# A long convolution's transform as 64 by 32 points in place of 128 by 16, with both parts of a split in one contraction

## The chip, the core and the metric

The kernel runs on one core of a Trainium2 chip. The core has engines with a queue of instructions each: TensorE (PE, matrix products; its weight loads are listed as PEld), VectorE (DVE), ScalarE (ACT), GpSimd (POOL) and SyncE (SP, which here only issues transfers). Each works through its queue in order and waits for the others by semaphores. The metric is the device time of one execution in microseconds; lower is better.

## What is computed

Four sublayers on x with S = 2048 rows and D = 576 columns, in fp32. Twice: a Fourier mixing, then a gated convolution.

```python
def _A_ref(x, dft_seq_re, dft_seq_im, dft_hid_re, dft_hid_im):
    a = einsum("bsd,ed->bse", x, dft_hid_re)
    b = einsum("bsd,ed->bse", x, dft_hid_im)
    return einsum("ts,bse->bte", dft_seq_re, a) - einsum("ts,bse->bte", dft_seq_im, b)

def _B_ref(q, k, v, shift_k, ssm_k, ssm_D):
    k_shift = ...          # short causal convolution of k, 4 taps per channel
    kv = k_shift * v
    y = irfft(rfft(pad(kv)) * rfft(pad(ssm_k)))[:, :S]   # causal, length 2S, per channel
    return q * (y + kv * ssm_D)

x = x + _A_ref(layernorm(x), ...)
x = x + _B_ref(layernorm(x), k, v, shift_k, ssm_k, ssm_D)
x = x + _A_ref(layernorm(x), ...)
x = x + _B_ref(layernorm(x), k, v, shift_k, ssm_k, ssm_D)
```

The filtered signal y depends on k, v, shift_k, ssm_k and ssm_D alone, not on x. It is computed once and used in both gated sublayers. In the text, this part is "the branch".

## The kernel before

**Precision.** A product of fp32 values is made of values rounded to a shorter form (`float32r`). An operand is split into a high part, rounded by ScalarE, and a low part, the rest, by VectorE (`split`, lines 93 to 95): one ScalarE copy and one VectorE subtraction. A product is then three matmuls: high by high, high by low and low by high.

**The main loop.** `layer` (lines 308 to 346) makes the first mixing as 128 steps: four blocks of 512 output columns (tb), real and imaginary part (g), 16 slices of rows (k). A step takes one 128x512 tile of the DFT matrix, the "c tile". `load_c` loads and splits it two steps ahead, into a ring of three tiles (`ring["cs"]`). The step then issues 12 matmuls of 512 columns into four accumulators (`s`) and two into a fifth (`rm`). For the first 16 steps, rows of x are normalised on the way (`get_x0`). At the end of a block's half, `evac_u` and `evac_r` take the accumulators to tiles u. Once both halves of a block are there, `hidden` (lines 274 to 297) makes the products with the matrices w, which `load_w` loads and splits from step 41 (`W_FROM`) on.

**The branch** runs in between, as a generator that the main loop advances (lines 798 to 823). It has three stages.

- *The first stage*, up to `f1_products`, transforms the zero-padded signals over 128 points spaced 16 rows apart, for each of the 16 phases j: once for the filter ssm_k (src 1), once for the product kv (src 0). That makes 32 row tiles of 128 partitions x 576 columns. `convolve` (lines 389 to 404) makes the shifted k for two phases at a time, seven VectorE operations on tiles of 1152 columns. `f1_split` (lines 433 to 443) multiplies by v for src 0 and splits the row tile into the ring xf of three tiles, that lie in the region `f1r` with the constants fc. `f1_products` (lines 445 to 456) makes, for each half of the columns (288) and for real and imaginary part, three matmuls into one of three PSUM banks `bk` and a ScalarE copy out, and then stores the two parts to t_d in memory. The products follow the splits by one or two row tiles (`F1_LAG`). From step 16 to step 42 (`F1_END`) about one row tile is taken per main step, and the convolution is issued at the pace at which its results fall due (lines 472 to 484).
- *The middle stage* reads t_d in 37 pieces, 128 rows by 504 columns for both signals (or the columns left over), transforms over the 16 phases with one 128x128 matrix, multiplies the two spectra, transforms back and stores to v_d. Its loads begin at step 45 (`MID_LOAD`), its products at step 47.
- *The second inverse stage* loads v_d by phase (`load_row`), splits it, and makes for each phase and each half of the columns six matmuls (`i2_products`), which go to the tensors yb_d.

After this, `make_x1` and `gated` use yb_d for both gated sublayers, and a second mixing follows with fewer block products.

**What sets the order.** Nothing is written out by hand: the tile framework puts the instructions of each engine in an order before the run, by readiness in a model of its own and by the place in the program. `behind` and `issue_after` only add "not ahead of that instruction on this engine". On the chip, every engine keeps that order. So a c tile's low half on VectorE can stand behind convolution work and splits of the branch, and a main step on TensorE cannot begin before its c tile's two halves are there.

Of the kernel before, what the change touches and what calls it, by code (L numbers as in the profile page):

```python
# [10 lines left out]
F32 = mybir.dt.float32  # L11
FR = mybir.dt.float32r
AF = mybir.ActivationFunctionType
OP = mybir.AluOpType

P = 128
S = 2048
D = 576
J = S // P
TB = 4  # L20
NT = 512
HD = D // 2
NC = 4
REM = D - NC * P
EPS = 1e-5
# [16 lines left out]
MW = 504  # L42
# [8 lines left out]
KP = 4  # L51
H = 2 * P
WIDE = 2 * NT
# [14 lines left out]
def fnet_h3_kernel(ctx: ExitStack, tc: tile.TileContext, x, c_mat, w_re, w_im, k_pad, v, shift_k,  # L68
                   ssm_k, ssm_d, f1c, i2c, midc, out):
    nc = tc.nc  # L70
# [3 lines left out]
    dr = ctx.enter_context(tc.tile_pool(name="dr", bufs=1, space=bass.MemoryType.DRAM))  # L74

    def mm(ps, lhsT, rhs, first, last, more=False):
        nc.tensor.matmul(ps, lhsT, rhs, start=first, stop=last, skip_group_check=more)  # L77
# [15 lines left out]
    def split(h, l, src):  # L93
        a = nc.scalar.activation(h, src, AF.Copy).ins  # L94
        return a, nc.vector.tensor_tensor(l, src, h.bitcast(F32), OP.subtract).ins  # L95
# [68 lines left out]
    anchor, made, rounded, pows, biased, halved, added, evac, parted, stored = [], [], [], [], [], [], [], [], [], []  # L164

    def load_after(dst, src):
        with tc.issue_after(anchor[-1]):
            return nc.sync.dma_start(dst, src).ins
# [31 lines left out]
        made.append(nc.vector.tensor_tensor(t[:, D + REM:], y[:, :NC * P], h[:, :NC * P], OP.subtract).ins)  # L200
        return t

    t_d = dr.tile([P, J, 2, 2, D], F32, name="t")
    v_d = dr.tile([P, J, 2, D], F32, name="vd")
    yb_d = [dr.tile([P, D], F32, name=f"yb{j}") for j in range(J)]
    xa_d = [dr.tile([P, D], F32, name=f"xa{j}") for j in range(J)]
    xb_d = [dr.tile([P, D], F32, name=f"xb{j}") for j in range(J)]
# [147 lines left out]
    def branch():  # L355
        f1r = region_b(FR, "f1r")
        lay(f1r, 0, ("xf", 2 * D, 3), ("fc", 4 * P, 5))
        at = lay(flts, SC_AT + CRAW * NT, ("so", D, 4), ("land", D, 3))
        lay(flts, at, ("craw", NT, 1))
        f1f = region_a(F32, "f1f")  # L360
        ks = f1f[:, :KR * 2 * D]
        lay(f1f, KR * 2 * D, ("wt", 2 * D, 2), ("rp", 2 * D, 2))
        tmp = f1f[:, 8 * 2 * D:]
        wt, rows, landed, fcs = [], {}, {}, {}
# [68 lines left out]
        def f1_split(j, src):  # L433
            r = landed.pop((j, src))
            if not src:
                row = rows[j // 2][:, j % 2, :]
                nc.vector.tensor_tensor(row, row, r, OP.mult)
                r = row
            elif j == 0:
                nc.vector.tensor_tensor(r[:1], r[:1], tmp[:1, D:], OP.add)  # L440
            xf = parts("xf")
            parted[:] = split(xf[0], xf[1], r)
            return xf

        def f1_products(j, src, xf, fc):
            for hf in range(2):
                so = two(ring["so"]())
                cs = slice(hf * HD, (hf + 1) * HD)
                for c in range(2):
# [4 lines left out]
                    stored[:] = [nc.scalar.activation(so[:, c, :], ps[:, :HD], AF.Copy).ins]  # L454
                nc.scalar.dma_start(t_d[:, j, :, src, cs], so)
                yield

        conv, made_ops, split_up, share = convolve(), 0, [], 0.0
        for n, (j, src) in enumerate(todo):
# [3 lines left out]
            xf = f1_split(j, src)  # L463
# [48 lines left out]

        RW = D - MW
        per = MW // RW
        groups = P // 4
# [6 lines left out]
        def load_mid(n):  # L522
            if n < len(mids):
                first, count = mids[n]
                w = width(n)
                landed[n] = [r[:, :w] for r in apart] if n % 2 else [ring["land"]()[:, :2 * w]]
                ends = landed[n] if n % 2 else [two(landed[n][0])[:, i] for i in range(2)]
                src = t_d[4 * first:4 * (first + count)]
                if n < groups:
                    src = src.rearrange("q j c s d -> (q j c) s d")[:, :, :MW]  # L530
                    if n % 2:
                        for i in range(2):
                            load_after(ends[i], src[:, i])
                    else:
                        load_after(two(landed[n][0]), src)
                else:
                    src = src.rearrange("(g q) j c s d -> (q j c) s g d", q=4)
# [41 lines left out]
        def mid_inverse(n, yf):  # L579
            w = width(n)  # L580
            pv = bank()
            mm(pv[:, :w], mc[:, 2, :], yf[0], True, False)
            mm(pv[:, :w], mc[:, 2, :], yf[1], False, False)
            mm(pv[:, :w], mc[:, 3, :], yf[0], False, True)
            vo = ring["vo"]()[:, :w]
            act(vo, pv[:, :w], AF.Copy)
            first, count = mids[n]
            dst = v_d[4 * first:4 * (first + count)]
            if n < groups:
                nc.scalar.dma_start(dst.rearrange("q j c d -> (q j c) d")[:, :MW], vo)  # L590
            else:
                nc.scalar.dma_start(dst.rearrange("(g q) j c d -> (q j c) g d", q=4)[:, :, MW:],
                                    vo.rearrange("p (g d) -> p g d", g=count))

        landed, halves, fcs = {}, {}, {}
# [48 lines left out]
        def i2_products(hf, j, fc, vf):  # L644
            yo = ring["vo"]()
            ps = bank()
            for c in range(2):
                cs = slice(c * D + hf * HD, c * D + (hf + 1) * HD)
                mm(ps[:, :HD], fc[:, c, :], vf[0][:, cs], c == 0, False)
                mm(ps[:, :HD], fc[:, c, :], vf[1][:, cs], False, False)  # L650
                mm(ps[:, :HD], fc[:, 2 + c, :], vf[0][:, cs], False, c == 1)
# [12 lines left out]
        for j in range(J):  # L664
            vf, fc = halves.pop(j), fcs.pop(j)
# [132 lines left out]
    for n, whole in layer(get_x0, lambda j: x[:, j, :], done0, pending):  # L798
        if (whole or whole is not None and n % J < J - 1) and n <= F1_END:
            at = n if whole else n - 0.5  # L800
# [27 lines left out]
        m = n - PREP  # L828
# [132 lines left out]
    cs, done = {}, []  # L961
# [68 lines left out]
    for n, whole in layer(get_x1, lambda j: xb_d[j], done1, pending, 1):  # L1030
# [42 lines left out]
    for ch in range(9):  # L1073
        first, then = (ch + 4, ch + 6) if ch < 4 else (12, ch + 15) if ch < 8 else (22, 24)
# [27 lines left out]
def _parts(a):  # L1102
    h = _r11(a)
    return h, _r11(a - h.astype(np.float64))


def _constants():
    p, q, j, r = np.arange(P), np.arange(P), np.arange(J), np.arange(J)
    n = (16 * p[None, :, None] + j[:, None, None]) * (4 * q[None, None, :] + 1) % 8192
    ang = 2 * np.pi * n / 8192  # L1110
    f1 = [_parts(np.cos(ang)), _parts(-np.sin(ang))]
    f1c = np.stack([f1[0][0], f1[1][0], f1[0][1], f1[1][1]], axis=2)
    at = ang.transpose(0, 2, 1)
    i2 = [_parts(np.cos(at) / S), _parts(-np.sin(at) / S)]
    i2c = np.stack([i2[0][0], i2[1][0], i2[0][1], i2[1][1]], axis=2)
    th = 2 * np.pi * (j[:, None] * r[None, :] % J) / J
    f2 = np.zeros((4, J, 2, 2, 4, J))
    i1 = np.zeros((2, 4, J, 4, J, 2))
    c, s = np.cos(th), np.sin(th)
    for a in range(4):  # L1120
        f2[a, :, 0, 0, a, :] = c
        f2[a, :, 1, 0, a, :] = s
        f2[a, :, 0, 1, a, :] = -s
        f2[a, :, 1, 1, a, :] = c
        i1[0, a, :, a, :, 0] = c.T
        i1[1, a, :, a, :, 0] = -s.T
        i1[0, a, :, a, :, 1] = s.T
        i1[1, a, :, a, :, 1] = c.T
    m = [*_parts(f2.reshape(P, P)), *_parts(i1.reshape(P, P))]
    return f1c, i2c, np.stack(m, axis=1)  # L1130


# [34 lines left out]
```

## Time and profile before

| | |
|---|---|
| median of 3 runs | 1190.47 us (1190.42 to 1191.18) |
| profiled execution | 1190.62 us, span of its instructions 1188.8 us |
| TensorE busy | 1172.7 us, 99% |
| VectorE busy | 814.3 us, 68% |
| ScalarE busy | 614.6 us, 52% |
| first and last product of the first stage | 6.8 and 199.4 us |
| granted TensorE clock | 0.999 |

In the rows of groups and of the timeline, a line stands for the source line of the kernel, then the engine, the operation and the tiles as output<-inputs. A tile of a region carries the region's name: the split rows and the constants of the first stage are `f1r`, c tiles are `mats`, their raw form `flts`, the convolution's tiles `f1f`. In a group, `xcount | busy, mean` is followed by the idle time of the engine just before these instructions and what ended it. In a timeline, the first number is the start and the second the duration, both in microseconds, and x6 means six instructions in a row. In a window, each engine has its busy microseconds and, in brackets, its instructions; then come the granted clock, the share of the DMA engines and GB/s.

### The profile page before, as it was taken

To read this page: it belongs to the slowest core of one execution; us is meant where nothing else is said; L and a number is where in the kernel's file an instruction comes from. 1 tells how busy PE (TensorE), PEld (TensorE's weight loads), DVE (VectorE), ACT (ScalarE), POOL (GpSimd) and SP (SyncE) were. 2 spreads that over 40 slices of the span, in tenths; PEclk is the share of its full clock that TensorE was granted. 3 is DMA by queue.
4 is the path that set the end of the run, shared out by engine and by line. 5 is a ranking of instruction groups with operands and counts; after the bars stand their busy time and mean duration, and the time that the engine had idled before them with its cause. 6 is when DMAs were issued, how large, how long until landed. Compare 5 with 4: busy or idle time off the path is not lost.

```text
span 1188.8 us, 17284 instructions
## 1 busy us (share of the span) xinstructions
PE 1172.7 (99%) x6077; PEld 1013.5 (85%) x6077; DVE 814.3 (68%) x1335; ACT 614.6 (52%) x1106; POOL 66.2 (6%) x100
## 2 busy tenths in 40 slices
PE   7999999999999999999999999999999999999997
PEld 6888888887788888889988898888888888889997
DVE  7899794677677677753447765874775776874764
ACT  7965665466656566644535656634434435540200
POOL 2200000000000000001101111000000000001111
PEclk9999999999999999999999999999999999999999
DMA  9889898545576546459957786872582597696621
GB/s 338 295 266 308 262 297 251 187 151 183 176 236 200 176 137 181 116 160 295 294 164 260 241 262 216 263 261 72 179 315 82 159 326 274 199 335 201 217 94 41
DMA packets 153770, 257.71 MB, mean 217 GB/s; under 512 B 27601, under 2 KB 68817, under 8 KB 153682
## 3 DMA queue, kind: packets, MB, share of 16 engines
q1 hardware_dynamic: 113074, 205.58, 53.7%
q10 hardware_dynamic: 36000, 42.63, 10.3%
q0 software_dynamic: 4608, 8.39, 2.6%
q8 instruction: 48, 0.79, 0.3%
q14 instruction: 40, 0.33, 0.1%
HBM read 189.89 MB, written 66.65 MB: 216 GB/s over the span
## 4 chain that ended last, share of the span: by engine, by line
PE 95%; DVE 2%; DMA 1%; ACT 1%; issue 0%; POOL 0%; POOLq 0%; SPq 0%; DVEq 0%; ACTq 0%
PE s L77 54%; PE bk L77 35%; PE rm L77 6%; DMA flts<-in_c_mat 1%; ACT flts L506 0%; DMA flts<-in_ssm_k 0%; DVE flts L183 0%; DVE u L95 0%; ACT mid L506 0%; DVE mats L95 0%; DVE mats L200 0%; ACT mats L197 0%; ACT u L94 0%; DVE mid L511 0%; POOL flts L186 0%
## 5 line engine op out<-in xcount | busy, mean ns | idle before, releaser
L77 PE MATMUL s<-mats 128*128 128x512 f32 x2088 | 524.1, 392 | 0.8 <-ACT mats L94 0.6
L77 PEld LDWEIGHTS s<-mats 128*128 128x128 f32 x2088 | 386.8, 188 | 79.8 <-DVE u L95 1.5
L95 DVE TENSOR_TENSOR mats<-flts,mats 128x512 fp32r<-128x512 f32 x201 | 137.5, 688 | 80.7 <-ACT mats L94 78.1
L94 ACT ACTIVATE mats<-flts 128x512 fp32r<-128x512 f32 x201 | 125.7, 627 | 102.5 <-PE bk L77 31.3
L506 ACT ACTIVATE flts<-bk 64x504 f32<-64x504 f32 (+3 forms) x180 | 99.0, 550 | 82.9 <-PE bk L77 76.4
L77 PEld LDWEIGHTS bk<-w,u 128*128 128x128 f32 x864 | 117.8, 188 | 4.7 <-ACT flts L506 1.3
L77 PE MATMUL bk<-w,u 128*128 128x288 f32 x864 | 120.5, 295 | 0.5 <-ACT flts L506 0.5
L77 PE MATMUL bk<-mid 128*128 128x504 f32 (+1 forms) x525 | 120.1, 356 | 0.7 <-ACT flts L506 0.2
L511 DVE TENSOR_TENSOR mid<-flts,mid 128x1008 fp32r<-128x1008 f32 (+3 forms) x90 | 80.3, 902 | 45.6 <-ACT mid L506 45.5
L77 PEld LDWEIGHTS bk<-mid 128*128 128x128 f32 x525 | 88.0, 188 | 16.7 <-ACT flts L506 1.8
L77 PE MATMUL rm<-mats 128*128 128x512 f32 x304 | 94.5, 390 | 0.0
L506 ACT ACTIVATE mid<-flts 128x1008 fp32r<-128x1008 f32 (+3 forms) x90 | 71.9, 799 | 37.2 <-DMA flts<-vd 14.2
L454 ACT ACTIVATE flts<-bk 128x288 f32<-128x288 f32 x128 | 50.7, 410 | 48.8 <-PE bk L77 48.3
L77 PE MATMUL bk<-f1r 128*128 128x288 f32 x384 | 64.7, 301 | 7.4 <-ACT f1r L94 6.8
L77 PEld LDWEIGHTS bk<-f1r 128*128 128x128 f32 x384 | 59.9, 192 | 13.9 <-ACT f1r L94 6.8
L77 PE MATMUL bk<-mats 128*128 128x288 f32 (+1 forms) x376 | 67.8, 317 | 0.0
L77 PEld LDWEIGHTS rm<-mats 128*128 128x128 f32 x304 | 57.0, 188 | 12.3
L77 PE MATMUL s<-t,mats 128*128 128x512 f32 x264 | 64.9, 389 | 0.0
L292 DVE TENSOR_TENSOR flts<-flts,bk 128x288 f32<-128x288 f32 x48 | 21.8, 453 | 61.5 <-PE bk L77 61.3
L77 PE MATMUL bk<-mats,t 128*128 128x288 f32 (+1 forms) x368 | 59.3, 303 | 0.0
L186 POOL TENSOR_TENSOR flts<-flts 128x1 f32<-128x1 f32 x35 | 30.1, 860 | 522.1 <-DVE flts L185 518.8
L77 PEld LDWEIGHTS bk<-mats 128*128 128x128 f32 x376 | 55.5, 188 | 3.4
(149 smaller groups left out, 1432.1 us busy)
## 6 DMA issues: line engine op xcount, KB each, us to landing
flts<-in_c_mat SPq DMA_DIRECT2D x148, 256.0 KB, 3.9
ph<-in_c_mat SPq DMA_DIRECT2D x54, 512.0 KB, 4.0
t<-flts ACTq DMA_DIRECT2D x64, 288.0 KB, 4.7
flts<-in_c_mat SPq DMA_DIRECT2D x30, 512.0 KB, 5.1
flts<-vd SPq DMA_DIRECT2D x16, 576.0 KB, 5.1
vd<-flts ACTq DMA_DIRECT2D x36, 252.0 KB, 2.9
flts<-t SPq DMA_DIRECT2D x16, 504.0 KB, 4.0
ud<-ph ACTq DMA_DIRECT2D x12, 512.0 KB, 5.3
```

Source lines behind the costliest of these rows:

```text
L77: nc.tensor.matmul(ps, lhsT, rhs, start=first, stop=last, skip_group_check=more)
L94: a = nc.scalar.activation(h, src, AF.Copy).ins
L95: return a, nc.vector.tensor_tensor(l, src, h.bitcast(F32), OP.subtract).ins
L186: pows.append(nc.gpsimd.tensor_tensor(rs, ve, mhalf, OP.pow).ins)
L292: added[:] = [nc.vector.tensor_tensor(rows[hf], rows[hf], ps[:, :HD], OP.add).ins]
L454: stored[:] = [nc.scalar.activation(so[:, c, :], ps[:, :HD], AF.Copy).ins]
L506: last_act.append(nc.scalar.activation(*args, **kw).ins)
L511: nc.vector.tensor_tensor(l, src, h.bitcast(F32), OP.subtract)
```

## The change

The transform of 2048 points is cut in 64 by 32 in place of 128 by 16. A row tile of 128 partitions now holds two phases, j and 16 + j, of 64 points each: the host lays out k, v and ssm_k so that the even groups of 16 rows lie in partitions 0 to 63 and the odd ones in 64 to 127 (`halves`). The contraction has 64 points, and the 128 rows of the matmul are filled with the high part of a phase and its low part. For each of the two phases b, a tile xf[b] holds the high part in the phase's own half of the partitions and the low part in the other half, and the constant's high part stands in both halves. One matmul so makes high by high and high by low. The second takes the constant's low part, and makes low by high and low by low. So `f1_products` has two matmuls per group, not three, and `f1_split` splits each half of the partitions by itself. Real and imaginary part come out in one product, as 64 frequencies x 2.

The middle stage transforms over 32 phases, on pieces of two frequencies in place of four, with the same tile sizes. In the second inverse stage the six matmuls stay; their constants are now half zeros, as each of the two phases fills 64 of the 128 output rows, and both are summed into one bank. The rows of v_d come in two runs per partition in place of one.

```diff
+Q = P // 2
...
-    t_d = dr.tile([P, J, 2, 2, D], F32, name="t")
-    v_d = dr.tile([P, J, 2, D], F32, name="vd")
+    t_d = dr.tile([Q, 2, 2 * J, 2, D], F32, name="t")
+    v_d = dr.tile([Q, 2, 2 * J, D], F32, name="vd")
...
-                nc.sync.dma_start(ks[:, at:at + 2 * D],
-                                  bass.AP(tensor=k_pad.tensor, offset=k_pad.offset + 2 * i * D,
-                                          ap=[[J * D, P], [1, 2 * D]]))
+                nc.sync.dma_start(two(ks[:, at:at + 2 * D]), k_pad[:, 2 * i:2 * i + 2, :])
...
             xf = parts("xf")
-            parted[:] = split(xf[0], xf[1], r)
+            for b in range(2):
+                here, there = (slice(0, Q), slice(Q, P)) if b == 0 else (slice(Q, P), slice(0, Q))
+                parted[:] = split(xf[b][here], xf[b][there], r[here])
             return xf
...
-                for c in range(2):
+                for b in range(2):
                     ps = bank()
-                    mm(ps[:, :HD], fc[:, c, :], xf[0][:, cs], True, False)
-                    mm(ps[:, :HD], fc[:, c, :], xf[1][:, cs], False, False)
-                    mm(ps[:, :HD], fc[:, 2 + c, :], xf[0][:, cs], False, True)
-                    stored[:] = [nc.scalar.activation(so[:, c, :], ps[:, :HD], AF.Copy).ins]
-                nc.scalar.dma_start(t_d[:, j, :, src, cs], so)
+                    mm(ps[:, :HD], fc[:, b, :], xf[b][:, cs], True, False)
+                    mm(ps[:, :HD], fc[:, 2 + b, :], xf[b][:, cs], False, True)
+                    stored[:] = [nc.scalar.activation(so[:, b, :], ps[:, :HD], AF.Copy).ins]
+                nc.scalar.dma_start(t_d.rearrange("q c (b j) s d -> (q c) j s b d", b=2)[:, j, src, :, cs], so)
...
-                load_after(landed[j], v_d[:, j].rearrange("p c d -> p (c d)"))
+                load_after(two(landed[j]), v_d.rearrange("q c (b j) d -> (q c) j b d", b=2)[:, j])
...
-            nc.scalar.dma_start(yb_d[j][:, hf * HD:(hf + 1) * HD], yo)
+            nc.scalar.dma_start(yb_d[j].rearrange("(p b) d -> b p d", b=2)[:, :, hf * HD:(hf + 1) * HD], yo)
```

The rest of the diff renames indices of the middle stage in the same way and builds the constants and the host layout for the new cut.

More of the change, by code (lines that the diff above doesn't have):

```diff
@@ L514, in branch @@
         per = MW // RW
-        groups = P // 4
+        groups = Q // 2
         mids = [(q, 1) for q in range(groups)] + [(q, min(per, groups - q)) for q in range(0, groups, per)]
@@ L527, in load_mid @@
                 ends = landed[n] if n % 2 else [two(landed[n][0])[:, i] for i in range(2)]
-                src = t_d[4 * first:4 * (first + count)]
+                src = t_d[2 * first:2 * (first + count)]
                 if n < groups:
-                    src = src.rearrange("q j c s d -> (q j c) s d")[:, :, :MW]
+                    src = src.rearrange("q c j s d -> (q c j) s d")[:, :, :MW]
                     if n % 2:
@@ L536, in load_mid @@
                 else:
-                    src = src.rearrange("(g q) j c s d -> (q j c) s g d", q=4)
+                    src = src.rearrange("(g q) c j s d -> (q c j) s g d", q=2)
                     for i in range(2):
@@ L587, in mid_inverse @@
             first, count = mids[n]
-            dst = v_d[4 * first:4 * (first + count)]
+            dst = v_d[2 * first:2 * (first + count)]
             if n < groups:
-                nc.scalar.dma_start(dst.rearrange("q j c d -> (q j c) d")[:, :MW], vo)
+                nc.scalar.dma_start(dst.rearrange("q c j d -> (q c j) d")[:, :MW], vo)
             else:
-                nc.scalar.dma_start(dst.rearrange("(g q) j c d -> (q j c) g d", q=4)[:, :, MW:],
+                nc.scalar.dma_start(dst.rearrange("(g q) c j d -> (q c j) g d", q=2)[:, :, MW:],
                                     vo.rearrange("p (g d) -> p g d", g=count))
@@ L646, in i2_products @@
             ps = bank()
[L647 to L651, printed above, removed]
+            for b in range(2):
+                cs = slice(b * D + hf * HD, b * D + (hf + 1) * HD)
+                mm(ps[:, :HD], fc[:, b, :], vf[0][:, cs], b == 0, False)
+                mm(ps[:, :HD], fc[:, b, :], vf[1][:, cs], False, False)
+                mm(ps[:, :HD], fc[:, 2 + b, :], vf[0][:, cs], False, b == 1)
             act(yo, ps[:, :HD], AF.Copy)
-            nc.scalar.dma_start(yb_d[j][:, hf * HD:(hf + 1) * HD], yo)
+            nc.scalar.dma_start(yb_d[j].rearrange("(p b) d -> b p d", b=2)[:, :, hf * HD:(hf + 1) * HD], yo)
         for j in range(3):
@@ L1107, in _constants @@
 def _constants():
-    p, q, j, r = np.arange(P), np.arange(P), np.arange(J), np.arange(J)
-    n = (16 * p[None, :, None] + j[:, None, None]) * (4 * q[None, None, :] + 1) % 8192
+    p, q, t = np.arange(Q), np.arange(Q), np.arange(2 * J)
+    n = (2 * J * p[None, :, None] + t[:, None, None]) * (4 * q[None, None, :] + 1) % 8192
     ang = 2 * np.pi * n / 8192
-    f1 = [_parts(np.cos(ang)), _parts(-np.sin(ang))]
-    f1c = np.stack([f1[0][0], f1[1][0], f1[0][1], f1[1][1]], axis=2)
+    f1 = _parts(np.stack([np.cos(ang), -np.sin(ang)], axis=-1).reshape(2, J, Q, P))
+    f1 = np.stack([*f1[0], *f1[1]], axis=2)
+    f1c = np.concatenate([f1, f1], axis=1)
     at = ang.transpose(0, 2, 1)
[L1114 to L1118, printed above, removed]
-    c, s = np.cos(th), np.sin(th)
[L1120 to L1128, printed above, removed]
+    i2 = _parts(np.stack([np.cos(at), -np.sin(at)], axis=2).reshape(2, J, P, Q) / S)
+    i2c = np.zeros((J, P, 4, 2, Q))
+    for b in range(2):
+        for m in range(2):
+            i2c[:, :, 2 * m + b, b] = i2[m][b]
+    i2c = i2c.reshape(J, P, 4, P)
+    th = 2 * np.pi * (t[:, None] * t[None, :] % (2 * J)) / (2 * J)
+    f2 = np.zeros((2, 2, 2 * J, 2, 2, 2 * J))
+    i1 = np.zeros((2, 2, 2 * J, 2, 2, 2 * J))
+    c, s = np.cos(th), np.sin(th)
+    for a in range(2):
+        f2[a, 0, :, 0, a, :] = c
+        f2[a, 1, :, 0, a, :] = s
+        f2[a, 0, :, 1, a, :] = -s
+        f2[a, 1, :, 1, a, :] = c
+        i1[0, a, :, a, 0, :] = c.T
+        i1[1, a, :, a, 0, :] = -s.T
+        i1[0, a, :, a, 1, :] = s.T
+        i1[1, a, :, a, 1, :] = c.T
     m = [*_parts(f2.reshape(P, P)), *_parts(i1.reshape(P, P))]
-    return f1c, i2c, np.stack(m, axis=1)
+    return tuple(v.astype(np.float32) for v in (f1c, i2c, np.stack(m, axis=1)))
 def kernel(**inputs):
@@ L1141, in perm, with halves @@
         return m.transpose(1, 4, 3, 2, 0)
+    def halves(m):
+        return m.reshape(Q, 2, *m.shape[1:]).transpose(1, 0, *range(2, m.ndim + 1)).reshape(m.shape)
     f1c, i2c, midc = _constants()
+    rows = J * np.arange(P)[:, None] + np.arange(J + 4)
     arrays = {
@@ L1148 @@
         "w_im": a["A_dft_hid_im"].T,
-        "k_pad": np.pad(a["B_k"][0], ((3, 1), (0, 0))),
-        "v": a["B_v"].reshape(P, J, D),
+        "k_pad": halves(np.pad(a["B_k"][0], ((3, 1), (0, 0)))[rows]),
+        "v": halves(a["B_v"].reshape(P, J, D)),
         "shift_k": np.broadcast_to(a["B_shift_k"].T, (P, 4, D)),
-        "ssm_k": a["B_ssm_k"].T.reshape(P, J, D),
+        "ssm_k": halves(a["B_ssm_k"].T.reshape(P, J, D)),
         "ssm_d": a["B_ssm_D"],
```

## The prediction

> **What bounds the kernel now.** I read the page's busy times first, then its chain, then the groups by shape, and then only the stage that the change touches.
>
> ```profile
> span 1188.8 us, 17284 instructions
> PE 1172.7 (99%) x6077; PEld 1013.5 (85%) x6077; DVE 814.3 (68%) x1335; ACT 614.6 (52%) x1106; POOL 66.2 (6%) x100
> PE 95%; DVE 2%; DMA 1%; ACT 1%; issue 0%; POOL 0%; POOLq 0%; SPq 0%; DVEq 0%; ACTq 0%
> ```
>
> TensorE bounds the kernel as a whole: 99% busy and 95% of the chain. VectorE's 68% is a mean over stages, so the stretch in which the first branch stage runs has to be looked at by itself. The windows give all engines, then the instructions on the tile f1r alone (f1r holds the split rows and constants of that stage):
>
> ```profile
> core 0: us, PE busy (x) PEld busy (x) DVE busy (x) ACT busy (x) POOL busy (x), PEclk, DMA share, GB/s
> 0.00:60.00 60.00, 52.57 (x239) 44.12 (x240) 47.76 (x125) 49.78 (x100) 15.40 (x24) 1.00 0.91 315
> 60.00:188.50 128.50, 128.50 (x686) 112.11 (x685) 114.98 (x138) 78.72 (x171) 6.40 (x12) 1.00 0.90 284
> ...
> 0.00:60.00 60.00, 11.07 (x54) 9.58 (x54) 3.77 (x5) 4.02 (x6) 2.37 (x4) 1.00 0.91 315
> 60.00:188.50 128.50, 48.18 (x296) 45.35 (x297) 20.25 (x27) 18.36 (x27) 5.87 (x11) 1.00 0.90 284
> ```
>
> From 60 to 188.5 us (the end of the last split on VectorE) TensorE is full, but VectorE is at 114.98 of 128.50, 89%. Five of the stage's 32 splits lie before 60 us and 27 behind it. VectorE's 13.5 idle microseconds there were spent so:
>
> ```profile
> DVE f1f L437 <- DMA flts<-in_v: 4.1, 2, 2.6
> DVE mats L95 <- ACT mats L94: 3.9, 3, 1.8
> DVE f1r L95 <- ACT f1r L94: 2.5, 3, 1.5
> DVE u L95 <- ACT u L94: 1.7, 3, 0.7
> DVE flts L703 <- POOL flts L681: 0.7, 1, 0.7
> ```
>
> The first three are waits of an engine that has run ahead: for a load into a ring that it frees itself, and for ScalarE halves that are held back until TensorE gives a c tile or xf tile free.
>
> **What goes.** Three matmuls per group become two: 32 row tiles x 4 groups = 128 fewer of the 384.
>
> ```profile
> L77 PE MATMUL bk<-f1r 128*128 128x288 f32 x384 | 64.7, 301 | 7.4 <-ACT f1r L94 6.8 <-ACT flts L454 0.7
> 131.98 0.95 PE L77 MATMUL bk<-f1r 128*128 128x288 f32 x6
> 132.77 1.54 PE L77 MATMUL s<-mats 128*128 128x512 f32 x6
> ```
>
> The 301 ns are one matmul's latency; its place in the stream is start to start: (132.77 - 131.98) / 6 = 0.132 us. So 128 x 0.132 = **16.9 us** of TensorE work go (1.4%). The remaining matmuls keep shape and 128 rows of contraction.
>
> **What comes.** Each row tile is split once for either half of the partitions: one ScalarE copy and one VectorE subtraction more, 32 of each, of 64 partitions and the same 576 columns. The trace has no 64x576 one; the nearest pairs of equal columns are the mid stage's:
>
> ```profile
> L568 DVE TENSOR_TENSOR flts<-bk,flts 64x504 f32<-64x504 f32 x36 | 24.3, 676 | 1.2
> L569 DVE TENSOR_TENSOR flts<-flts 128x504 f32<-128x504 f32 x36 | 24.6, 682 | 1.0
> L506 ACT ACTIVATE flts<-bk 64x504 f32<-64x504 f32 x108 | 63.0, 583 | 19.3 <-PE bk L77 18.0
> L506 ACT ACTIVATE flts<-bk 128x504 f32<-128x504 f32 x36 | 21.3, 591 | 29.1 <-PE bk L77 26.7 <-DMA vd<-flts 2.2
> ```
>
> Half the partitions take the same time (L568 also reads one half of the partitions and writes the other, as the new subtraction does). So an added one costs a full slot, which I take start to start where the next follows at once:
>
> ```profile
> 82.09 0.74 DVE L95 TENSOR_TENSOR f1r<-flts,f1r 128x576 fp32r<-128x576 f32 x1
> 82.76 1.34 DVE L403 TENSOR_TENSOR f1f<-f1f 128x1152 f32<-128x1152 f32 x1
> 48.62 0.68 ACT L94 ACTIVATE f1r<-f1f 128x576 fp32r<-128x576 f32 x1
> 49.20 0.68 ACT L197 ACTIVATE mats<-early 128x576 fp32r<-128x576 f32 x1
> ```
>
> VectorE: 32 x 0.67 = **21.4 us**. ScalarE: 32 x 0.58 = 18.6 us. Bounds: half a slot if partitions counted (10.7 us), the full 0.75 us duration otherwise (24 us). I keep 0.67.
>
> **What moves at no cost.** The t rows, the mid loads and stores and the yb stores keep their sizes and runs, only in another order. The v_d row load falls from one run of 4608 bytes per partition to two of 2304:
>
> ```profile
> flts<-vd SPq DMA_DIRECT2D x16, 576.0 KB, 5.1
> flts<-t SPq DMA_DIRECT2D x16, 504.0 KB, 4.0
> 525.00:615.00 90.00, 90.00 (x553) 82.51 (x552) 34.95 (x39) 40.03 (x65) 6.88 (x13) 1.00 0.79 251
> ```
>
> The 504 KB load already goes in runs of 2016 bytes and lands in 4.0 us, so I take nothing; bounds are -1 and +1 us each. TensorE was never idle in the second inverse stage that uses them (90.00 of 90.00), as other matmuls fill it; without that cover 16 x 1 us would show. The second inverse stage keeps its matmuls: its stationary tiles are half zeros, and zeros are streamed like anything else. The k_pad load has the same bytes per partition.
>
> **The sum goes by VectorE.** Up to 60 us: 18 matmuls fewer (-2.4 us), 5 splits more (+3.4 us on VectorE, +2.9 us on ScalarE, which is 49.78 of 60 busy with the normalisation of x). The first product now also waits for VectorE:
>
> ```profile
> 6.05 0.68 ACT L94 ACTIVATE f1r<-flts 128x576 fp32r<-128x576 f32 x1 [1.16 <-DMA flts<-in_ssm_k]
> 6.76 0.76 DVE L95 TENSOR_TENSOR f1r<-flts,f1r 128x576 fp32r<-128x576 f32 x1 [0.99 <-ACT f1r L94]
> 6.78 2.60 PE L77 MATMUL bk<-f1r 128*128 128x288 f32 x9 [6.78 <-ACT f1r L94]
> ```
>
> I take 1.0 us late at 60 us (bounds -2.4 and +3.4). Then VectorE needs 114.98 + 27 x 0.67 = 133.1 us, and the waits that are not its own doing stay: 1.7 for the evacuation of u and 0.7 for GpSimd. The last split ends at 61.0 + 133.1 + 2.4 = **196.5 us** instead of 188.5. TensorE's own work in this stretch shrinks by 296 / 3 x 0.132 = 13.0 us to 115.5, so it must wait some 20 us there less what it may run ahead: the c tiles allow two steps beyond the one running, and the products lag two items.
>
> What ends after the last split decides. Now:
>
> ```profile
> 187.71 0.76 DVE L95 TENSOR_TENSOR f1r<-f1f,f1r 128x576 fp32r<-128x576 f32 x1 [1.53 <-ACT f1r L94]
> 190.30 0.69 DVE L95 TENSOR_TENSOR mats<-flts,mats 128x512 fp32r<-128x512 f32 x1 [1.83 <-ACT mats L94]
> 195.84 0.69 DVE L95 TENSOR_TENSOR mats<-flts,mats 128x512 fp32r<-128x512 f32 x1
> ...
> 197.98 1.75 PE L77 MATMUL bk<-f1r 128*128 128x288 f32 x12
> 199.56 2.90 PE L77 MATMUL s<-mats 128*128 128x512 f32 x12
> ...
> 202.76 2.88 PE L77 MATMUL s<-mats 128*128 128x512 f32 x12
> ...
> 205.93 2.88 PE L77 MATMUL s<-mats 128*128 128x512 f32 x12
> ```
>
> Before, all products and the main steps 43 and 44 are done at 205.93. Now two products (16 x 0.132 = 2.1 us) follow the last split. If steps 43 and 44 were done while TensorE waited, that point is 196.5 + 2.1 = 198.6, a gain of 7.3; if both still follow (205.93 - 199.56 = 6.4 us), it is 205.0, a gain of 0.9. The queue above has the c halves of steps 43 and 44 behind the last split, so I stay nearer the lower end: **3 us gained** of 16.9. The profiled run took 1190.62 us (0.15 above the median 1190.47): 1190.6 - 3.0 = **1187.6 us**. This case's own range, with the bounds at 60 us, is 1180 to 1192. Next late would be the w halves, whose last one on VectorE starts at 209.97, ahead of the first hidden product at 212.28:
>
> ```profile
> 209.97 0.82 DVE L107 SCALAR_TENSOR_TENSOR w<-flts,w 128x576 fp32r<-128x576 f32 x1 [1.12 <-ACT w L106]
> 212.28 0.95 PE L77 MATMUL bk<-w,u 128*128 128x288 f32 x6
> ```
>
> A gain above about 2 us meets them, and is kept only if main steps fill in.
>
> **Rivals.** *The queue as it stands, slower.* If the waits do not shrink so far (5.5 us stay instead of 2.4) and the start is 3.4 late, the last split ends at 60 + 3.4 + 133.1 + 5.5 = 202.0; the c half of step 43 comes 0.6 behind it, then 2.1 of products and 6.4 of steps: 211.1 against 205.93, so 5.2 slower, 1195.8. With this order it turns to a loss once the last split ends after 205.93 - 9.1 = 196.8, only 0.3 behind my forecast. For it: every VectorE instruction waits behind the one ahead of it, and the added pair stands ahead of c halves that TensorE needs. Against it: the c halves could be queued first.
>
> *All of it saved:* 1173.7. It needs 133.1 us of VectorE work in 115.5 us. Only splits at half price (27 x 0.33, 124 us in all), with work shifted behind the stage, come near it. The 64-row pairs speak against that.
>
> *The waits also cost clock.* The first nine products took 2.60 us where 9 x 0.132 = 1.19 is the later pace: 1.4 us lost after the 6.78 idle microseconds of the start (part of it the wait for the low half). The 13.9 us of lost saving hold two such idle pieces: 2 x 1.4 = 2.8 us, so 1190.4. For it: that row. Against it: the granted clock is 1.00 in every stretch, and the waits should come in many small pieces, one per c half. The Trainium skill, "TensorE: Matmul & The Clock Gate", section "HAM oscillation — how this bites in real kernels", asks for no TensorE gaps above about 3.4 us, as the half clock returns behind them; by that figure it could be four pieces and 5.6 us (an estimate), a change paid back by its own waits. The trace agrees at the start and has no second case.
>
> **How the numbers follow.** Forecast 0.48, slower queue 0.33, all saved 0.10, clock 0.05, something else 0.04. A measurement of this kernel tells about 0.2%, 2.4 us, from no change, so "same" is 1188.1 to 1192.9. The forecast case gives 0.28 faster, 0.18 same, 0.02 slower; the slower queue 0.05 same and 0.28 slower; all saved 0.10 faster; the clock 0.03 same and 0.02 slower; the rest 0.02 faster and 0.02 slower. Together 0.40 faster, 0.26 same, 0.34 slower. The range 1180 to 1197 reaches over the forecast's own and the slower queue, and leaves out most of "all saved" and the far end of the losses.
>
> **What would show it.** TensorE products on f1r: 256, at 0.132 apart inside a block. VectorE splits on f1r: 64, at 0.67 a slot. VectorE over 95% busy from 60 us to the last split, which ends near 196; TensorE idle there for the first time, released by VectorE's c or f1r halves, some 14 us. Wrong if VectorE still idles there while TensorE is full (all saved), or if 64-row splits take under 0.5 us; wrong in sign if the last split ends after 200.

## The result and the profile after

The changed kernel takes 1263.8 us (median of 4 runs, 1263.34 to 1265.16) against 1190.45 us of the kernel before: 1.0617 times as long, 95% interval 1.0598 to 1.0635. The prediction was 1187.6 us, in a range from 1180 to 1197.

The page of the kernel after, the same three lines as of before:

```profile
span 1262.2 us, 17104 instructions
PE 1187.9 (94%) x5949; PEld 1009.6 (80%) x5949; DVE 842.4 (67%) x1367; ACT 635.0 (50%) x1138; POOL 66.0 (5%) x100
PE 46%; ACTq 2%; DMA 2%; ACT 1%; issue 0%; DVE 0%; POOLq 0%; DVEq 0%
```

TensorE has 128 matmuls less (5949, not 6077) and is yet 15 us longer busy; it idles for 74 us. The shares of the chain add up to 51% only: it could be followed back to 599 us and no further, so TensorE's 46% is not to be set beside the 95% of before. ACTq, the queue in which ScalarE issues transfers, had 0% before and has 2% here.

To see where the time went, both traces are cut at 60 us and then at the same events: the last split of the first stage, the first and the last store to yb. Windows of the kernel after, columns as in the prediction:

```profile
60.00:208.30 148.30, 133.20 (x630) 107.10 (x629) 142.94 (x176) 102.18 (x210) 8.02 (x13) 0.97 0.77 246
208.30:551.30 343.00, 337.58 (x1671) 283.35 (x1670) 235.76 (x354) 205.58 (x347) 2.11 (x4) 1.00 0.58 179
551.30:683.50 132.20, 96.86 (x494) 83.62 (x492) 28.66 (x31) 32.63 (x55) 6.86 (x13) 0.86 0.50 154
683.50:1262.00 578.50, 570.88 (x2952) 496.73 (x2952) 387.20 (x688) 245.30 (x432) 35.27 (x48) 0.99 0.63 209
```

and of the kernel before, whose stretch from 60 to 188.5 us the prediction shows:

```profile
188.50:534.50 346.00, 344.06 (x1712) 289.75 (x1711) 236.09 (x354) 207.68 (x349) 2.12 (x4) 1.00 0.57 176
534.50:611.80 77.30, 77.30 (x485) 71.43 (x484) 28.48 (x31) 33.40 (x56) 6.88 (x13) 1.00 0.84 266
611.80:1188.00 576.20, 570.23 (x2963) 496.09 (x2961) 387.04 (x688) 245.01 (x432) 35.36 (x48) 1.00 0.63 209
```

By stage: the first branch stage 148.3 in place of 128.5 (+19.8), the middle stage 343.0 for 346.0 (-3.0), the stage of the yb stores 132.2 for 77.3 (**+54.9**), the rest +2.3. Three quarters of the loss lie in a stage that the prediction had taken as unchanged. There, VectorE, ScalarE and GpSimd are busy for nearly the same time in both kernels (28.7, 32.6 and 6.9 us), and the DMA share has fallen from 0.84 to 0.50. So none of these does more; something waits. The instructions on the tile yb, first before, then after (duration of the issue in ns, min/median/max):

```profile
L653 ACTq DMA_DIRECT2D yb<-flts x32: 326/326/348, 534.5 to 611.5; - x32
```

```profile
L653 ACTq DMA_DIRECT2D yb<-flts x32: 488/2798/7811, 551.3 to 680.6; - x32
```

The same 32 stores of 144 KB hold ScalarE's queue for 2.8 us (median) in place of 0.33. What stands behind one is seen in the timeline after (start, duration, engine, line):

```profile
573.63 4.23 ACTq L653 DMA_DIRECT2D yb<-flts  x1
577.97 0.63 ACT L95 ACTIVATE mats<-flts 128x512 fp32r<-128x512 f32 x1 [4.36 <-issue]
578.63 0.69 DVE L96 TENSOR_TENSOR mats<-flts,mats 128x512 fp32r<-128x512 f32 x1 [5.45 <-ACT mats L95]
...
586.94 1.06 PE L78 MATMUL bk<-mid 128*128 128x288 f32 x6 [1.23 <-ACT flts L506]
```

ScalarE sits idle for 4.36 us until its queue has the store out; the c tile's halves and the evacuation of banks come late. What TensorE waits for on record is the evacuation, and what ScalarE waits for most is its own queue (engine, line, what ended the wait, us in total, times, longest us; then one piece of the chain):

```profile
PE bk L78 <- ACT flts L506: 29.5, 10, 6.1
ACT flts L506 <- issue: 33.1, 8, 6.4
600.32 18.23 DMA yb<-flts
```

The last line is one store, 18.2 us from its issue to its landing, where the median before was 3.9. And TensorE is slower besides: the granted clock of the stage is 0.86, and nearly the same work (494 matmuls for 485) keeps it busy for 96.9 us, not 77.3. Of the 54.9 us, 35.3 are waiting (132.2 - 96.9) and 19.6 longer busy time. The clock was at half for 37.5 us of the stage, and TensorE was busy in 30.1 of them, so some 15 of the 19.6 us go to the clock (an estimate).

The first stage, on VectorE and TensorE of the kernel after:

```profile
139.28 1.54 DVE L96 TENSOR_TENSOR f1r<-flts,f1r 64x576 fp32r<-64x576 f32 x2
140.85 1.36 DVE L402 TENSOR_TENSOR f1f<-f1f 128x1152 f32<-128x1152 f32 x1
...
149.68 0.75 DVE L96 TENSOR_TENSOR f1r<-flts,f1r 64x576 fp32r<-64x576 f32 x1
150.46 1.36 DVE L397 TENSOR_TENSOR f1f<-f1f 128x1152 f32<-128x1152 f32 x1
...
153.61 0.75 DVE L436 TENSOR_TENSOR f1f<-f1f,flts 128x576 f32<-128x576 f32 x1
154.28 1.35 DVE L397 TENSOR_TENSOR f1f<-f1f 128x1152 f32<-128x1152 f32 x1
...
157.79 2.48 DVE L96 TENSOR_TENSOR u<-s,u 128x512 fp32r<-128x512 f32 x4
158.53 2.08 PE L78 MATMUL s<-mats 128*128 128x512 f32 x4 [8.57 <-DVE u L96]
```

VectorE is 96% busy (142.94 of 148.30), as forecast, but the last split ends at 208.2 us, not at 196.5. A halved split takes 0.78 us from its start to the next (150.46 - 149.68), as does each of the two at 139.28; the 128x576 operation at 153.61 takes 0.67, at the same duration of 0.75. TensorE idles for 15.1 us (148.3 - 133.2). Its longest wait, 8.57 us, is for the evacuation of u, which stands behind convolution work and splits in VectorE's queue, and from 151.7 to 162.0 us the granted clock is at half.

### The profile page after: what moved, and what is told of

It reads as the page before. It is cut to its first block, busy times and chain, and to the rows that moved or that the text cites. A ratio compares the mean times of both kernels' runs of the same rounds, so it can differ in the third digit from the quotient of the medians.

```text
span 1262.2 us, 17104 instructions
## 1 busy us (share of the span) xinstructions
PE 1187.9 (94%) x5949; PEld 1009.6 (80%) x5949; DVE 842.4 (67%) x1367; ACT 635.0 (50%) x1138; POOL 66.0 (5%) x100
## 3 DMA queue, kind: packets, MB, share of 16 engines
q0 software_dynamic: 4608, 8.39, 2.6%
## 4 chain that ended last, share of the span: by engine, by line
PE 46%; ACTq 2%; DMA 2%; ACT 1%; issue 0%; DVE 0%; POOLq 0%; DVEq 0%
PE s L78 29%; PE bk L78 15%; ACTq L653 2%; PE rm L78 2%; DMA yb<-flts 1%; DMA flts<-vd 1%; ACT mid L506 0%; ACT flts L506 0%; DVE mid L511 0%; POOLq L1172 0%; DVE u L96 0%; ACT u L95 0%; DVE ph L696 0%; DVE flts L184 0%; DVE ph L293 0%
## 5 line engine op out<-in xcount | busy, mean ns | idle before, releaser
L78 PE MATMUL s<-mats 128*128 128x512 f32 x2088 | 543.2, 400 | 21.5 <-DVE u L96 14.9
L78 PEld LDWEIGHTS s<-mats 128*128 128x128 f32 x2088 | 395.2, 193 | 108.4 <-DVE u L96 16.3
L78 PE MATMUL bk<-mid 128*128 128x504 f32 (+1 forms) x525 | 128.0, 372 | 32.7 <-ACT flts L506 28.7
L78 PEld LDWEIGHTS bk<-mid 128*128 128x128 f32 x525 | 92.2, 200 | 53.6 <-ACT flts L506 34.2
L78 PE MATMUL rm<-mats 128*128 128x512 f32 x304 | 97.7, 395 | 0.0
L454 ACT ACTIVATE flts<-bk 128x288 f32<-128x288 f32 x128 | 47.6, 406 | 26.5 <-PE bk L78 13.9
L78 PE MATMUL bk<-f1r 128*128 128x288 f32 x256 | 50.5, 308 | 9.9 <-DVE f1r L96 9.7
L78 PEld LDWEIGHTS bk<-f1r 128*128 128x128 f32 x256 | 42.7, 192 | 20.9 <-DVE f1r L96 11.7
```

Of the source, the lines that this page charges most:

```text
L454: stored[:] = [nc.scalar.activation(so[:, b, :], ps[:, :HD], AF.Copy).ins]
```

## The experiments

Two theories at first. **A**: the store to yb is slow to issue since its outermost dimension is 2, and it blocks ScalarE. **D**: in the first stage VectorE's added time is the loss. The rivals were the other things that the change does in the same stages.

**e1: rows in order.** The constants' columns are interleaved, so that the plain store is back.

```diff
-    i2c = np.zeros((J, P, 4, 2, Q))
+    i2c = np.zeros((J, P, 4, Q, 2))
-            i2c[:, :, 2 * m + b, b] = i2[m][b]
+            i2c[:, :, 2 * m + b, :, b] = i2[m][b]
-            nc.scalar.dma_start(yb_d[j].rearrange("(p b) d -> b p d", b=2)[:, :, hf * HD:(hf + 1) * HD], yo)
+            nc.scalar.dma_start(yb_d[j][:, hf * HD:(hf + 1) * HD], yo)
```

> The changed kernel with the columns of the second inverse constants interleaved, so that the 128 output rows come out in the order of memory and the store to yb is again one run of rows, as before the change. All else stays: two products, halved splits, v_d rows in two runs. Theory A (the store's outermost dimension of 2 makes it slow to issue and blocks ScalarE's queue): the stage from the first to the last yb store falls from 132.2 back to about 77 us, and the whole to 1263.8 - 55 = about 1209, with the yb issues at 0.33 us each. Rival B (the two-run loads of v_d, or the half-zero constants, slow that stage): it stays near 1263. In both the first stage keeps its loss of some 17 us, as VectorE is full there.

Measured: 1211.2 us, ratio 1.0181 (1.0161 to 1.0202). The issues are back at 0.33 us (median). The stage of the stores, in this run:

```profile
549.80:632.80 83.00, 79.02 (x489) 72.02 (x488) 28.46 (x31) 33.23 (x55) 6.86 (x13) 1.00 0.80 248
```

52.6 us of the 73.4 are the store's, and the clock is 1.00 again. The stage still has 5.7 us more than before.

**e2: the store alone**, in the kernel before: its store line is that of the change, and its constants' columns are put in the matching order.

```diff
+    i2c = i2c.reshape(J, P, 4, P // 2, 2).transpose(0, 1, 2, 4, 3).reshape(J, P, 4, P)
-            nc.scalar.dma_start(yb_d[j][:, hf * HD:(hf + 1) * HD], yo)
+            nc.scalar.dma_start(yb_d[j].rearrange("(p b) d -> b p d", b=2)[:, :, hf * HD:(hf + 1) * HD], yo)
```

> The kernel before with the columns of its second inverse constants put in the order evens, odds, and the store to yb rearranged as in the change (outermost dimension 2). Nothing else is changed. Theory A: the store alone costs about 55 us, so 1190 + 55 = 1245, with issues of 2 to 8 us on ScalarE's queue. Rival B: within 5 us of 1190.

Measured: 1245.9 us (one run), 55 above the kernel before. The issues take 2.79 us (median). The stage of the stores here:

```profile
533.50:665.10 131.60, 96.18 (x493) 82.76 (x491) 28.60 (x31) 32.23 (x55) 6.88 (x13) 0.88 0.50 154
```

131.6 us with nearly the same busy times and a clock as low: one changed access pattern, with the order of rows that it needs, makes the whole of it.

**e3: two stores**, one for each half of the partitions, in the changed kernel.

```diff
+            for b in range(2):
+                nc.scalar.dma_start(yb_d[j].rearrange("(p b) d -> b p d", b=2)[b, :, hf * HD:(hf + 1) * HD], yo[b * Q:(b + 1) * Q])
```

> The changed kernel with each yb store cut in two, one for each half of the partitions: 64 runs each, to every second row of memory. Theory A in the form that the outermost dimension of 2 is what hurts: the issues are short again (0.33 us, 64 of them), the stage is near 77 us and the whole near e1, 1209 to 1214. Rival C (runs that lie 4608 bytes apart in memory are slow by themselves): the issues stay at microseconds and the whole near 1263.

Measured: 1208.5 us (one run); 64 issues of 0.50 us (median), short again, if not the 0.33 us expected. The rows go to the same places in memory, 4608 bytes apart, so the rival C falls: it is not the spacing but that both halves are in one instruction. No run issued the stores from another engine, so it is open how much of the 55 us is the blocked queue of ScalarE and how much the slow transfers themselves.

**e12 and e13: outermost dimension 4 and 8**, as e2 with 4 and 8 in place of 2.

> The kernel before with the store to yb cut 4 by 32 (outermost dimension 4) in place of 128 rows in order, the constants' columns in the matching order. By the outermost dimension as the number of DMA engines that share the store: 32 runs on each of 4 engines where the two-run form had 64 on each of 2, so half as long: issues of about 1 us, and a loss of at most half of 55, some 5 to 27 us: 1195 to 1217. Rival (any order of rows but the natural one costs the same): 1246. The Trainium skill, DMA: Bandwidth & Descriptors, section Why a DMA increments its semaphore by 16 and not by 1, gives that number as the largest up to 16 that divides the slowest dimensions of both sides.

> The same with an outermost dimension of 8: 16 runs on each of 8 engines. By that theory the issues are nearly short (0.33 to 0.6 us) and the whole is 1190 to 1195. Rival (any other order costs the same): 1246.

Measured: 1201.3 and 1191.7 us (one run each, 1189.9 for the kernel before beside them). The issues of the two runs:

```profile
L653 ACTq DMA_DIRECT2D yb<-flts x32: 512/527/2225, 533.0 to 621.3; - x32
```

```profile
L653 ACTq DMA_DIRECT2D yb<-flts x32: 580/590/1187, 534.1 to 612.4; - x32
```

The loss is 55, 11 and 2 us for 2, 4 and 8; the last is no more than single runs of the kernel before differ (1188.7 to 1192.9). The median issue with 4 is 0.53 us, not about 1 as expected, but its longest is 2.2.

The number of packets on ScalarE's queue changes too. The kernel before, e2, e12 and e13 (packets, MB, share of 16 engines):

```profile
q10 hardware_dynamic: 36000, 42.63, 10.3%
q10 hardware_dynamic: 35552, 42.62, 9.8%
q10 hardware_dynamic: 35616, 42.62, 10.2%
q10 hardware_dynamic: 35744, 42.62, 10.4%
```

With 2, 4 and 8 there are 448, 384 and 256 packets fewer, that is 14, 12 and 8 for each of the 32 stores, all of under 512 bytes; in e3, where 32 stores more are issued, there are 512 more (36512), 16 for each. So a plain store has 16 small packets beside its rows, and the three forms have 2, 4 and 8.

The Trainium skill, "DMA: Bandwidth & Descriptors", section "Why a DMA increments its semaphore by 16 and not by 1", states that a transfer runs on the largest number of DMA engines up to 16 that divides the slowest dimension of both sides. By that the plain store has 16 engines and the change's has 2, with 64 rows each. The order 2, 4, 8 agrees, and so do the packet counts, if each engine that takes part adds one small packet; no row names a single engine, so that reading is not shown by itself. It was a rule that spoke against this change, and the prediction did not weigh it.

**e6: one-run loads.** On top of e1, the middle stage's inverse constants give the rows of v_d phase by phase, so that a partition's row is one run of 4608 bytes again.

```diff
-                load_after(two(landed[j]), v_d.rearrange("q c (b j) d -> (q c) j b d", b=2)[:, j])
+                load_after(landed[j], v_d[:, :, 2 * j:2 * j + 2].rearrange("q c b d -> (q c) (b d)"))
...
+    by_phase = t.reshape(2, J).T.reshape(-1)
-        i1[0, a, :, a, 0, :] = c.T
+        i1[0, a, :, a, 0, :] = c.T[:, by_phase]
```

> The run with the rows of yb in order, and besides the columns of the middle stage's inverse constants put in such an order that a row of v_d comes in one run of 4608 bytes again. Theory F (the two-run load costs what this stage still lost, 83.0 against 77.3 us from the first to the last yb store): the stage returns to 77 us and the whole to 1211.2 - 5.7 = about 1205.5. Rival: the stage keeps 81 to 83 us and the whole 1209 to 1211, the load being hidden and the rest an effect of another order.

Measured: 1207.5 us, 1.0155 (1.0133 to 1.0177), 3.6 below e1 by the medians. The stage is back:

```profile
549.50:627.20 77.70, 77.70 (x486) 71.77 (x485) 29.29 (x31) 33.45 (x55) 6.86 (x13) 1.00 0.85 265
```

The intervals of e1 and e6 overlap, so the 3.6 us are not sharp; the stage's 5.3 us in the profiles (83.0 to 77.7) are the better evidence that the two-run load did cost. The median time from issue to landing of that load is 5.6 us in e1 and 3.8 in e6. What is left, 17 us, arises ahead of this stage: the first yb store comes at 549.5 us, not 534.5, and the last split ends at 207.9, not 188.5.

**e5: halved splits alone**, in the kernel before.

```diff
-            parted[:] = split(xf[0], xf[1], r)
+            for b in range(2):
+                rows_b = slice(b * P // 2, (b + 1) * P // 2)
+                parted[:] = split(xf[0][rows_b], xf[1][rows_b], r[rows_b])
```

> The kernel before, with each row tile of the first stage split in two halves of 64 partitions, to the same tiles and the same partitions: 32 more ScalarE copies and 32 more VectorE subtractions of 64 x 576, three products as before. Theory D (the loss in the first stage is VectorE's added time alone): the last split ends 15 to 20 us later than 188.5 and the whole is 1190 + 12 to 19 = 1202 to 1209. Rival E (the loss comes from what else the change does there: low parts written across the halves, first products that wait for both engines, another order): 1190 to 1196.

Measured: 1203.1 us, 1.0119 (1.0094 to 1.0143). The last split ends at 205.0 us (188.5 before). Windows of this run:

```profile
0.00:60.00 60.00, 50.71 (x228) 41.34 (x229) 47.60 (x122) 49.17 (x96) 14.25 (x22) 1.00 0.89 308
60.00:205.00 145.00, 138.57 (x715) 118.31 (x713) 140.30 (x174) 102.84 (x210) 8.06 (x13) 0.98 0.81 251
```

VectorE is at 140.30 of 145.00 with all 384 matmuls still there, and ScalarE at 102.84: the halved splits alone lengthen the stage by 16.5 us, with VectorE as the full engine. Theory D holds.

**e4: two products alone**, in the kernel before, with its splits.

```diff
-                    mm(ps[:, :HD], fc[:, c, :], xf[1][:, cs], False, False)
-                    mm(ps[:, :HD], fc[:, 2 + c, :], xf[0][:, cs], False, True)
+                    mm(ps[:, :HD], fc[:, 2 + c, :], xf[1][:, cs], False, True)
```

> The kernel before with two products per group in place of three and the splits as before; it leaves out the cross products of the first stage, so only its time counts. It measures what the removed matmuls are worth by themselves: 128 x 0.132 = 16.9 us if TensorE is the only bound, so 1173.6; VectorE has 115 us of work in a stretch that shrinks to 115.5 us, so part of it may be lost: 1174 to 1180. Rival: the stage is paced by its VectorE work already, and the gain is under 5 us, 1186 to 1190.

Measured: 1181.7 us against 1190.0, 0.9925 (0.9909 to 0.9942). Half of the 16.9 us are had; both theories' figures missed, on either side. The stage up to the last split, now 122.7 us:

```profile
60.00:182.70 122.70, 119.70 (x590) 100.26 (x589) 114.28 (x139) 75.83 (x174) 6.39 (x12) 0.99 0.90 289
```

VectorE is 93% busy and TensorE idles for 3.0 us, 2.0 of them for the evacuation of u on VectorE. In the whole profile, TensorE's busy time falls by 12.0 us (1172.7 to 1160.7) and its idle time grows by 4.5: even without any added work, part of the saving goes to waits. Why the busy time falls by less than 16.9 us stays open.

**e14: both edits without the crossing**, e4 and e5 together: low parts stay in their own half.

> The kernel before with both edits of the first stage at once, halved splits in their own partitions and two products per group; it leaves out the cross products, so only its time counts. What differs from the repaired change (1207.5) is only that low parts stay in their half and that a group's first product needs the high part alone. Theory D (VectorE's work sets the stage, the matmuls removed under it are worth nothing and even let the other waits show): 1201 to 1208, like the halved splits alone (1203.1) or the repaired change. Rival E (the crossing and the earlier need of the low part cost the rest): 1203.1 less 8.3, the gain of two products alone, that is 1193 to 1197.

Measured: 1204.2 us, 1.0123 (1.0106 to 1.0140); the last split ends at 204.3. That is the time of the halved splits alone: with VectorE full, the removed matmuls are worth nothing. Rival E falls for the most part. What the crossing, and all else that e6 still has of the change, adds is the 3.3 us to e6 by the medians; the intervals overlap, so it stays open.

**e7 and e8: work to GpSimd**, on top of e6. e7 gives it the second half's subtraction from the ninth row tile on, e8 the 16 products with v.

```diff
+                engine = nc.gpsimd if b and n > 7 else nc.vector
+                l = engine.tensor_tensor(low, r[here], high.bitcast(F32), OP.subtract).ins
```

```diff
-                nc.vector.tensor_tensor(row, row, r, OP.mult)
+                nc.gpsimd.tensor_tensor(row, row, r, OP.mult)
```

> The run with one-run loads, and besides the second half's low part made by GpSimd from the ninth row tile on (24 subtractions of 64 x 576 leave VectorE). Theory D (VectorE's queue is what takes the saving): the last split ends 24 x 0.77 = 18 us earlier, near 190, and the whole comes to 1182 to 1192, faster than before if the two-product run's 8.9 us can be had. Rival: GpSimd takes over 2 us for one, or its queue stands behind the constants' loads, which wait up to 18 us for TensorE, so that xf tiles come late: no better than the run without it, 1203 to 1215.

> The run with one-run loads, and besides the 16 products with v (128 x 576) made by GpSimd in place of VectorE. Theory D: 16 x 0.67 = 10.7 us leave VectorE, the last split ends near 198 and the whole is 8 to 11 us below the run without it, 1195 to 1198. Rival as for the low parts: GpSimd's own time and queue make it no better, 1203 to 1215.

Measured: 1223.0 us, 1.0277 (1.0259 to 1.0296), and 1221.0 us, 1.0261 (1.0243 to 1.0279): 15 and 13 us worse than e6, and worse than the rival had it. Theory D's gain is not had this way: in e7 VectorE is still busy for 151.1 of the 161.4 us from 60 us to the last split. Groups of e7 from 60 to 200 us, and one of the kernel before (60 to 188.5 us) to compare with:

```profile
L446 POOL TENSOR_TENSOR f1r<-flts,f1r 64x576 fp32r<-64x576 f32 x10 | 19.6, 1955 | 23.5 <-ACT f1r L444 21.2 <-DVE f1f L436 1.5 <-PE bk L78 0.9
L397 DVE TENSOR_TENSOR f1f<-f1f 128x1152 f32<-128x1152 f32 x22 | 35.6, 1620 | 0.1
```

```profile
L398 DVE TENSOR_TENSOR f1f<-f1f 128x1152 f32<-128x1152 f32 x22 | 29.5, 1349 | 0.1
```

GpSimd takes 1.96 us for one, and VectorE's own operations become longer beside it, 1.62 for 1.35 us. The Trainium skill, "SBUF — State Buffer", section "Who interferes with whom", says that a VectorE instruction with two SBUF inputs contends with a GpSimd instruction that reads SBUF. The rows agree.

**e10 and e11: another pacing.** F1_END = 44 in place of 42, in e6 and in the kernel before. In both, w is laid over the convolution's region two steps too early for this pacing, which changes the values of the branch; only their times count.

> The run with rows in order and one-run loads, and besides the first stage paced to end at main step 44 in place of 42, so that VectorE's branch work is mixed with two more steps' c halves. Theory D (VectorE's sum of work sets when the last split ends, but TensorE may have more main steps behind it by then): the last split stays near 208 and the whole falls by up to two steps, 2 x 3.2 = 6.4 us: 1201 to 1206. Rival: the wait only moves to the loading of the middle stage, 1206 to 1210.

> The kernel before with the same new pacing, as the control: TensorE is full in its first stage, so nothing is to be had, 1189 to 1193; or the later start of the middle stage costs the time of two steps, up to 1197.

Measured: 1211.6 us, 1.0175 (1.0157 to 1.0192), and 1191.6 us, 1.0007 (0.9996 to 1.0018). No gain in either, and 1211.6 us is above what both sides expected of e10: its last split still ends near 210 us, so this spreading of VectorE's work did not help.

No version of the change beats the kernel before. The only faster run, e4, leaves out products.

## Why the prediction was wrong

Point by point, by its own steps.

- **"What moves at no cost ... the yb stores keep their sizes and runs, only in another order."** This step failed, and it is three quarters of the loss: 52.6 us (e1), 55 alone (e2). The sizes and runs were indeed kept, but they are not the whole price of a transfer: the outermost dimension fell from 128 to 2. The prediction compared bytes and runs and had no row for that shape; it should have bounded it as an unknown. The issuing engine was ScalarE, so each slow issue stood in front of c halves and bank evacuations.
- **"The v_d row load ... I take nothing; bounds are -1 and +1 us each."** The stage paid 5.3 us in the profiles for 16 loads, 0.33 us each, within the bounds (by the landing times, 5.6 us in e1 stands against 5.1 before and 3.8 in e6). But it was not hidden, as said: TensorE waited 4.0 us in e1's stage (83.0 - 79.0).
- **16.9 us of TensorE work go.** The count and the slot came out (256 matmuls, 0.13 us apart), but only 8.3 us of it could be had in the kernel before (e4), and nothing once VectorE is full (e14 against e5).
- **VectorE 21.4 us, at 0.67 a slot.** The mechanism was right, the size too small. Half the partitions do cost the full duration, 0.75 us, but the slot is longer, 0.78: the next operation, of whatever kind, does not begin in the end of a halved split. The prediction took the slot of a 128-row split, and it priced only the 32 added ones, while the 32 old ones are halved too: 64 x 0.78 - 32 x 0.67 = 28.5 us, above its bound of 24. The trace before could have told: the 64-row operations of its pair (L568) take 0.71 us from start to start and the 128-row ones (L569) 0.60, at equal durations of 0.68. What makes the slot longer is not shown; e5, where low parts stay in their half, has 0.74 to 0.79.
- **"I take 1.0 us late at 60 us."** Too little: work on x, and two operations of the convolution, were moved behind 60 us. With this and the 54 longer slots, about half each, VectorE's busy time from there was 142.9, not 133.1, and its idle time 5.4, not 2.4. So the last split ended 11.7 us later than forecast.
- **"3 us gained."** Failed through the last two: by the prediction's own point, the sign turns once the last split ends after 196.8 us; it ended at 208.2. The rival "the queue as it stands, slower" was the true one for this stage, with 17 us (e6) and not 5.2. TensorE's idle time there was near the forecast (15.1 us, not some 14), but more than half of it was the one wait for u, not many small ones for c and f1r halves.
- **The clock rival** was right in kind and stood at the wrong place. In the stage of the stores the granted clock fell to 0.86, some 15 us by the estimate above. In the first stage it was 0.97, in one piece of 10 us in which TensorE was busy for 3.5: under 2 us, against the rival's 2.8.

## What to carry to other kernels

When a layout changes, put beside bytes and run lengths the outermost dimension of each transfer on both sides, and the engine that issues it: a store that is slow to issue stops all that stands behind it there. The order wanted in memory could be had here for nothing in the constants of the product that makes it, as e1 and e6 did.

Taking work from the engine that bounds the whole kernel gained half of it, 8.3 of 16.9 us, in a stage where another engine was at 89%, and nothing once the edit had filled that engine: first ask for that stage's second busiest engine, and price what the edit adds to it. Here 16.9 us off TensorE were paid with some 28 us on VectorE. And take the slot of an operation, start to start, from the same shape as its duration.

## What the runs showed of the hardware

- One 144 KB store with outermost dimension 2 holds the issuing queue for 2.8 us (median, up to 7.8); with 4 for 0.53 (up to 2.2), with 8 for 0.59 (up to 1.2), in order of rows 0.33. Such a store has 2, 4, 8 and 16 small packets beside its rows.
- A stage in which TensorE waits 35 of 132 us in pieces of some microseconds ran at a granted clock of 0.86; the same work without the waits at 1.00.
- On VectorE, a 64x576 subtraction takes as long as a 128x576 one, 0.75 us, but its slot from start to start is 0.78, not 0.67.
- A 64x576 subtraction in fp32 takes GpSimd 1.6 to 2.0 us, and VectorE's 128x1152 operations beside it took 1.62 in place of 1.35.
